# Attention nine pairs a group, and the eighth group's second product from seven products of quarters

## The chip, the cores and the metric

The kernel runs on one core of one Trainium2 chip. The metric is the device time of one execution in microseconds (us). Before the change it is 911.19 us, the median of three runs (911.01 to 911.4).

## The reference

Windowed attention (8 batches, 8 heads, 576 positions, head size 64), and then a SiLU MLP on its 4608 rows of 512 columns:

```python
scores = np.where((rel >= 0) & (rel < 128), q @ k.T / 8 + bias, -1e9)     # per batch and head
attn = exp(scores - max) / (sum + 1e-9)
x = (attn @ v).transpose(0, 2, 1, 3).reshape(4608, 512)
h = x @ w_in                      # 512 -> 2048
out = (h / (1 + exp(-h))) @ w_out # 2048 -> 512
```

## The kernel before

**Precision.** A float32 operand is carried as two fp16 parts (high and low), and a product is three matmuls: high by high, high by low, low by high. Such a matmul has a 128x128 block as its stationary operand and 512 columns as its moving operand.

**Groups and blocks.** The 4608 rows are nine groups of 512 (`g` from 0 to 8; "the eighth group" is `g` = 7). The 2048 hidden columns are 16 blocks of 128 (`f`); `n = 16 g + f` numbers all blocks. For each `n`, `gemm1` writes a PSUM tile `h` (12 matmuls), `act1` takes its tanh on ScalarE, `act2` forms the SiLU in the tile `gt` on VectorE, `act3` makes the high part `gh` on ScalarE, `act4` the low part `gl` on VectorE, and `gemm2` adds the block's share to four PSUM tiles `o` (12 matmuls). After the last block `store` sends the four tiles out.

**Steps.** `gemm1` and `gemm2` are cut into halves of six matmuls. Such a half is a step; a group has 64 steps. In this order the program issues for a block n: the two halves of `gemm1(n)`, then the two halves of `gemm2(n - 1)`. A table `plan`, filled by `put(step, function, ...)`, says what else is issued ahead of each step; `rank` sorts the work of one step. Each engine then runs its own queue strictly in the order in which the program issued it, and waits where a tile isn't ready.

**Attention.** A pair is half of the heads (four) for 128 rows; there are 72 pairs, p = 0 to 71, and a group needs eight of them before its MLP can begin. `at(p)` is the step at which pair p's `scores` are issued on TensorE. VectorE takes the row maxima (`row_max`, four instructions that also add the bias) in the next step, ScalarE the exponentials (`exps`) and their high part `hr` (`p_hi`), VectorE the low part (`p_lo`); two DMA transposes on SyncE's queue (`p_transpose`, tile `hl`) turn them, and `attend` is issued on TensorE 12 or 13 steps after the scores. `normalize` (three VectorE instructions), `x_hi` and `x_lo` follow, and `x_dma` transposes the finished rows `x`. From pair 36 on, q and k come as float32 (`load_qk16`, tile `r`, 512 KB) and are split by `hi16` on ScalarE and `lo16` on VectorE. Scores and attend share two PSUM buffers, called "a". In the pairs from 18 on `at(p)` is 8 steps a pair.

**Statistics.** The scale of each batch pair b = 2, 3 is taken from the data ahead of its first attention pair: nine blocks of v (`vscale_load`, `vscale_reduce` on VectorE) and nine of q and k (`qk_load`, `qk_sum`: two ScalarE sums each). Then `vscale_finish` runs in three stages.

**The last group.** The group in `FAST` takes its second product by seven products of quarters instead of eight (`gemm2_fast`): 512 rows by 128 hidden columns are seen as 2 x 2 quarters, which need sums and differences of activations (`act_sums`, three VectorE instructions per block) and of weights (`sum_float`, `sum_make`, `sum_hi`, `sum_lo`: eight blocks, mostly on GpSimd, in `SUMS_STEP` = 14 steps a block from step `SUMS` = 332). A block n is then 24 matmuls of 256 columns in `gemm1_fast` and 21 of 256 columns in `gemm2_fast`; `join_products` combines and `store_fast` sends out. Its `LAG` is two blocks: `gemm2(n - 2)` follows `gemm1(n)`. All other groups drain at their last block: `gemm2` of blocks 14 and 15 both run before the next group's first `gemm1`, with `turn_over` making `gh` and `gl` at once.

## Time and profile before

| | |
|---|---|
| median of three runs | 911.19 us |
| the profiled execution, its own time | 911.29 us |
| its span, first to last instruction | 909.5 us |
| TensorE (PE) busy | 900.5 us of the span |
| VectorE (DVE) busy | 718.6 us |
| ScalarE (ACT) busy | 582.9 us |
| GpSimd (POOL) busy | 180.8 us |

The 1.8 us between span and time lie around the program. Times in the rows are microseconds from the span's start, and nanoseconds where a mean of one instruction is given. PE's matmuls overlap their ends; the pace of a stream is read from one start to the next.

### The profile page before, as it was taken

The numbers are of one execution on the slowest core, as the hardware profiler recorded it, in microseconds if no ns is written. First come the engines' busy times: TensorE is split into PE (matmuls) and PEld (weight loads), VectorE is DVE, ScalarE is ACT, GpSimd is POOL, SyncE is SP. The second block draws the span as 40 slices with busy tenths as digits, with TensorE's granted clock in tenths as the row PEclk, the third lists the DMA queues.
The fourth block names the chain that finished last, engine by engine and source line by source line (L and its number), as shares of the span: only waits on it lengthen the run. The fifth ranks groups of instructions, "written<-read, shape, count | busy, mean of one in ns | idle before, by whom it ended". The sixth has DMA issues, their size and how long they took to land.

```text
span 909.5 us, 17946 instructions
## 1 busy us (share of the span) xinstructions
PE 900.5 (99%) x6761; PEld 570.0 (63%) x6761; DVE 718.6 (79%) x1734; ACT 582.9 (64%) x1184; POOL 180.8 (20%) x191
## 2 busy tenths in 40 slices
PE   9999999999999999999999999999999999999998
PEld 7877776888855555555555555555555555547887
DVE  6998998787988886767788888988988876655675
ACT  7789986675567755556577766666766666533342
POOL 2356662000000000000000004555654200000000
PEclk9999999999999999999999999999999999999999
DMA  8979824333386645434798736434655454311000
GB/s 324 395 178 258 242 55 132 71 93 71 82 234 162 184 117 125 112 90 116 171 248 204 197 93 155 105 93 105 163 116 117 116 154 107 78 35 59 1 25 24
DMA packets 198182, 122.94 MB, mean 135 GB/s; under 512 B 166480, under 2 KB 167632, under 8 KB 198096
## 3 DMA queue, kind: packets, MB, share of 16 engines
q1 hardware_dynamic: 197664, 121.41, 51.1%
q8 instruction: 53, 0.87, 0.4%
q10 hardware_dynamic: 432, 0.39, 0.1%
q14 instruction: 33, 0.27, 0.1%
HBM read 71.96 MB, written 9.44 MB: 89 GB/s over the span
## 4 chain that ended last, share of the span: by engine, by line
PE 81%; DVE 4%; ACT 2%; issue 1%; DVEq 0%; ACTq 0%
PE o L951 32%; PE h L754 30%; PE h L726 5%; PE av L584 4%; PE m L858 4%; PE sp L479 3%; PE sp L486 2%; PE h L759 1%; DVE hr L534 1%; DVE gt L787 1%; ACT gh L818 1%; DVE gl L832 1%; DVE t L510 1%; ACT t L520 0%; DVE x L155 0%
## 5 line engine op out<-in xcount | busy, mean ns | idle before, releaser
L754 PE MATMUL h<-xt,w 128*128 128x512 f16 (+1 forms) x1536 | 311.9, 353 | 0.0
L951 PE MATMUL o<-w,gh 128*128 128x512 f16 (+1 forms) x1024 | 311.1, 385 | 0.8 <-ACT gh L814 0.6
L783 ACT ACTIVATE gt<-h,tsc 128x512 f32<-128x512 f32 x128 | 87.7, 685 | 210.0 <-PE h L754 196.8
L754 PEld LDWEIGHTS <-w 128*128 128x128 f16 x1536 | 143.3, 98 | 123.1 <-issue 2.4
L951 PE MATMUL o<-w,gl 128*128 128x512 f16 (+1 forms) x512 | 196.3, 383 | 0.4 <-DVE gl L832 0.2
L787 DVE SCALAR_TENSOR_TENSOR gt<-gt,h 128x512 f32<-128x512 f32 x144 | 98.4, 684 | 79.1 <-ACT gt L783 78.5
L951 PEld LDWEIGHTS <-gh 128*128 128x128 f16 x768 | 74.6, 98 | 89.1 <-ACT gh L818 1.1
L520 ACT ACTIVATE t<-t,mx 128x256 f32<-128x256 f32 (+1 forms) x288 | 125.6, 485 | 7.4 <-DVE mx L510 7.2
L832 DVE SCALAR_TENSOR_TENSOR gl<-gt,wcut,gh 128x512 f16<-128x512 f32 x96 | 80.2, 835 | 52.4 <-ACT gh L818 51.6
L455 POOL TENSOR_SCALAR v<-rv,vsc 128x512 f16<-128x512 f32 x30 | 25.4, 848 | 471.1 <-DMA rv<-v 347.7
L534 DVE SCALAR_TENSOR_TENSOR hr<-t,hr 128x512 f16<-128x512 f32 (+1 forms) x128 | 97.0, 767 | 2.4 <-ACT hr L529 2.3
L818 ACT ACTIVATE gh<-gt,wcut 128x512 f16<-128x512 f32 x96 | 69.2, 721 | 39.0 <-DVE gt L787 36.1
L529 ACT ACTIVATE hr<-t 128x512 f16<-128x512 f32 (+1 forms) x128 | 71.3, 595 | 1.9 <-DMA hl<-hr 1.9
L951 PEld LDWEIGHTS <-gl 128*128 128x128 f16 x384 | 37.6, 98 | 46.7 <-DVE gl L832 1.8
L584 PEld LDWEIGHTS <-hl 128*128 128x128 f16 x1464 | 52.1, 98 | 15.9 <-issue 4.9
L510 DVE CUSTOM_DVE_ANT_0 t<-sp,tab,vsc 128x256 f32<-128x256 f32 (+1 forms) x144 | 58.5, 461 | 0.7
L584 PE MATMUL av<-v,hl 128*128 128x65 f16 (+1 forms) x1464 | 54.9, 193 | 1.7 <-DVE mx L510 1.0
L951 PEld LDWEIGHTS o<-w,gh 128*128 128x128 f32 x256 | 46.0, 188 | 10.3 <-issue 1.0
L510 DVE CUSTOM_DVE_ANT_0 t<-sp,tab 128x256 f32<-128x256 f32 (+1 forms) x144 | 50.1, 403 | 2.6 <-PE sp L486 2.3
L153 POOL TENSOR_TENSOR w<-wm,w 128x512 fp32r<-128x512 f32 x32 | 44.3, 1384 | 2.6
L759 PE MATMUL h<-xh,w 128*128 128x512 f32 x128 | 44.5, 404 | 0.0
L726 PE MATMUL h<-xt,w 128*128 128x256 f16 x384 | 44.2, 273 | 0.0
(193 smaller groups left out, 1232.3 us busy)
## 6 DMA issues: line engine op xcount, KB each, us to landing
r<-qk SPq DMA_DIRECT2D x36, 512.0 KB, 4.1
qs<-qk SPq DMA_DIRECT2D x18, 512.0 KB, 5.0
wr<-w_in SPq DMA_DIRECT2D x16, 512.0 KB, 6.8
wr<-w_out SPq DMA_DIRECT2D x16, 512.0 KB, 6.4
out<-ot SPq DMA_DIRECT2D x32, 256.0 KB, 2.6
rv<-v SPq DMA_DIRECT2D x30, 256.0 KB, 4.1
vm<-v SPq DMA_DIRECT2D x27, 256.0 KB, 4.7
q<-qk SPq DMA_DIRECT2D x18, 256.0 KB, 3.6
```

What stands on the lines that cost most here:

```text
L510: nc.vector.tensor_tensor_reduce(out=st[p]["t"][u][:, h, 2 * P - n :], in0=st[p]["sp"][h][:, u, o].rearrange("p o c -> p (o c)"), in1=tab[ ...
L520: nc.scalar.activation(x, x, AF.Exp, bias=st[p]["mx"][:, 2 * u + h : 2 * u + h + 1], scale=-1.0)
L529: nc.scalar.activation(split_of(p, u, hr)[:, 0], t[:, :, 2 * P - n :], AF.Copy, scale=PSCALE)
L534: nc.vector.scalar_tensor_tensor(out=hr[:, 1], in0=t[:, :, 2 * P - n :], scalar=PSCALE, in1=hr[:, 0], op0=ALU.mult, op1=ALU.subtract)
L584: nc.tensor.matmul(av[:, 2 * u + h, : rhs.shape[-1]], lhs, rhs, start=(n == 0), stop=(n == len(seq) - 1), skip_group_check=True,)
L726: nc.tensor.matmul(out, w[:, wp, cc], xt[g, "g"][:, 2 * t : 2 * t + 2, xp * NCC + cc], start=half == 0 and i == 0, stop=i == len(seq) - 1, ...
L754: nc.tensor.matmul(o, w[:, wp, cc], x, start=start and k == 0, stop=stop, skip_group_check=True)
L783: nc.scalar.activation(gt, hps[n], AF.Tanh, scale=scale)
L787: nc.vector.scalar_tensor_tensor(out=gt, in0=gt, scalar=1.0, in1=hps[n], op0=ALU.add, op1=ALU.mult)
L818: nc.scalar.activation(gh, gt, AF.Copy, scale=cut_of(n))
L832: nc.vector.scalar_tensor_tensor(out=gl, in0=gt, scalar=cut_of(n), in1=f32(gh) if n // NF < OUT16 else gh, op0=ALU.mult, op1=ALU.subtract)
L951: nc.tensor.matmul(ops[ti], a[:, t], w, start=(f == 0 and i == 0), stop=(f == NF - 1 and i == len(seq) - 1), skip_group_check=True,)
```

## The change

`FAST` gets the eighth group as well. Attention from pair 18 on runs nine pairs a group, at steps of seven (`PACE`, `EACH`); attend comes 10 steps after the scores (11 for a group's ninth pair). So attention ends in the seventh group. The weight sums start at step 240 instead of 332. The statistics of b = 2 and 3 stand at steps of four from 127 and 197 (`BOUNDS`, `FINISH`), and their nine reductions of v move from VectorE to ScalarE. Output tiles go to other buffers.

```diff
-FINISH1 = (37, 42, 45)
+FINISH = {1: (37, 42, 45), 2: (166, 168, 170), 3: (236, 239, 241)}
+BOUNDS = {2: 127, 3: 197}
-FAST = (NG - 1,)
+FAST = (NG - 2, NG - 1)
-SUMS, SUMS_STEP = 332, 14
+SUMS, SUMS_STEP = 240, 14
+OUT_TAGS = {3: ("w1_14", "w1_9"), 4: ("w1_13", "w1_14"), 6: ("w1_0", "w1_1")}
+PACE, EACH = 7, 9
...
-    return STEP * (p - 2 * GT) - LEAD
+    if p < 4 * GT + 2:
+        return STEP * (p - 2 * GT) - LEAD
+    g, k = divmod(p - 4 * GT - 2, EACH)
+    return (g + 1) * SLICE * NF + 2 + PACE * k
...
-        if b > 1 or b == 0 and i % 2:
+        if b == 0 and i % 2:
             nc.vector.tensor_reduce(m, t, axis=AX.XY, op=ALU.max, apply_absolute_value=True)
...
-            if n // NF == NG - 1:
-                act_sums(n)
+            act_sums(n)
...
-            a = n + (15 if p < 4 * GT else 13 if i < QK16 * NBLK else 12)
+            a = n + (15 if p < 4 * GT else 13 if p < 4 * GT + 2 else 11 if (p - 4 * GT - 2) % EACH == EACH - 1 else 10)
...
+        for b in range(QK16, NBB):
+            n = BOUNDS[b] + 4 * i
+            put(n, vscale_load, b, i)
+            put(n + 1, qk_load, b, i)
+            put(n + 4, vscale_reduce, b, i)
+            put(n + 6, qk_sum, b, i)
-            put(LOAD1[i // 2] if b == 1 else n - 53 + 5 * i, vscale_load, b, i)
-                put(n - 52 + 5 * i, qk_load, b, i)
-                put(n - 46 + 5 * i, qk_sum, b, i)
```

SyncE's queue around the transposes of pairs 48 and 49, before the change (`hl48_0` is the transposed probabilities of pair 48, `r16_51` the raw q and k of pair 51):

```order
L542 DMA_TRANSPOSE hl48_0_6913<-hr48_0_6887 128x8x128
L542 DMA_TRANSPOSE hl48_1_6953<-hr48_1_6910 128x8x128
L411 DMA r16_51_6966<-qk16 128x1024
L653 DMA_TRANSPOSE xt20_6029<-x23_6812 128x8x128
L542 DMA_TRANSPOSE hl49_0_7070<-hr49_0_7058 128x8x128
```

The same place after the change:

```order
L418 DMA r16_51_6763<-qk16 128x1024
L549 DMA_TRANSPOSE hl48_0_6782<-hr48_0_6736 128x8x128
L549 DMA_TRANSPOSE hl48_1_6797<-hr48_1_6779 128x8x128
L660 DMA_TRANSPOSE xt20_6205<-x23_6667 128x8x128
L418 DMA r16_52_6918<-qk16 128x1024
L549 DMA_TRANSPOSE hl49_0_6941<-hr49_0_6891 128x8x128
```

The raw load of a pair three later has moved from behind a pair's two transposes to ahead of them.

VectorE's queue in the stretch in which GpSimd makes the weight sums, before the change (`gt84` and `gl84` are `act2` and `act4` of block 84, `t52` the scores with bias of pair 52):

```order
L787 SCALAR_TENSOR_TENSOR gt84_7434<-gt84_7434,h84_7411 128x512
L832 SCALAR_TENSOR_TENSOR gl84_7452<-gt84_7434,wcut_3034,gh84_7451 128x512
L155 SCALAR_TENSOR_TENSOR x25_7455<-xs50_7421,x25_7455 128x256
L510 ISA t52_0_7495,mx52_7484<-sp52_0_7466,tab_65,vsc2_4578 128x256
L510 ISA mx52_7484 128x1
L510 ISA t52_1_7497,mx52_7484<-sp52_0_7466,tab_65,vsc2_4578 128x256
```

In that stretch after the change, at block 70 and pair 48:

```order
L794 SCALAR_TENSOR_TENSOR gt70_6703<-gt70_6703,h70_6671 128x512
L517 ISA t48_0_6706,mx48_6696<-sp48_0_6678,tab_65,vsc2_4448 128x256
L517 ISA mx48_6696 128x1
L517 ISA t48_1_6708,mx48_6696<-sp48_0_6678,tab_65,vsc2_4448 128x256
L517 ISA mx48_6696 128x1
L517 ISA t48_0_6706,mx48_6696<-sp48_1_6679,tab_65,vsc2_4448 128x256
L517 ISA mx48_6696 128x1
L517 ISA t48_1_6708,mx48_6696<-sp48_1_6679,tab_65,vsc2_4448 128x256
L517 ISA mx48_6696 128x1
L435 SCALAR_TENSOR_TENSOR q16_49_6645<-r16_49_6469,vsc2_4448,q16_49_6645 64x512
L838 SCALAR_TENSOR_TENSOR gl70_6722<-gt70_6703,wcut_3090,gh70_6721 128x512
```

Before, scores always fell on the same place within a block's four steps; with steps of seven they take all four places in turn. Here `act4` has moved away from `act2`, behind the four row maxima and a `lo16`.

## Rows read from the trace of the kernel before

**Rows 1.** The page: engines' busy time, and PE's granted clock in 40 slices.
```profile
PE 900.5 (99%) x6761; PEld 570.0 (63%) x6761; DVE 718.6 (79%) x1734; ACT 582.9 (64%) x1184; POOL 180.8 (20%) x191
...
PEclk9999999999999999999999999999999999999999
```

**Rows 2.** The page: the chain that ended last, by engine.
```profile
PE 81%; DVE 4%; ACT 2%; issue 1%; DVEq 0%; ACTq 0%
```

**Rows 3.** PE's own waits from the third to the eighth group, with their releasers.
```profile
PE o L951 <- ACT gh L818: 0.2, 1, 0.2
PE o L951 <- DVE gl L832: 0.2, 1, 0.2
```

**Rows 4.** Timeline of PE at the eighth group's end (start, us, what).
```profile
818.30 2.75 PE L754 MATMUL h<-xt,w 128*128 128x512 f16 x12
820.89 0.59 PE L951 MATMUL o<-w,gh 128*128 128x512 f16 x2
...
823.48 0.59 PE L951 MATMUL o<-w,gh 128*128 128x512 f16 x2
824.16 0.39 PE L951 MATMUL o<-w,gl 128*128 128x512 f16 x1
```

**Rows 5.** Timeline of the ninth group: the first product of two blocks in succession.
```profile
865.95 2.78 PE L726 MATMUL h<-xt,w 128*128 128x256 f16 x24
...
870.87 2.78 PE L726 MATMUL h<-xt,w 128*128 128x256 f16 x24
```

**Rows 6.** Busy time in windows: weight sums, fifth group, eighth group, twelve blocks of the ninth.
```profile
core 0: us, PE busy (x) PEld busy (x) DVE busy (x) ACT busy (x) POOL busy (x), PEclk, DMA share, GB/s
557.40:718.20 160.80, 160.38 (x1157) 83.44 (x1155) 141.01 (x294) 106.44 (x208) 84.92 (x84) 1.00 0.49 116
445.40:542.00 96.60, 96.60 (x711) 51.05 (x710) 79.14 (x204) 67.76 (x143) 2.93 (x4) 1.00 0.75 194
...
732.80:826.30 93.50, 93.42 (x649) 47.92 (x648) 59.95 (x145) 48.06 (x89) 2.80 (x3) 1.00 0.38 94
836.40:895.30 58.90, 58.90 (x542) 52.80 (x540) 41.20 (x83) 24.45 (x40) 0.00 (x0) 1.00 0.03 10
```

**Rows 7.** Timeline of SyncE's queue: the transposes of two pairs.
```profile
625.46 2.63 SPq L542 DMA_TRANSPOSE hl<-hr  x2
...
755.31 2.58 SPq L542 DMA_TRANSPOSE hl<-hr  x2
```

**Rows 8.** Timeline of PE: the attends that read them.
```profile
632.85 0.89 PE L584 MATMUL av<-v,hl 128*128 128x65 f16 x24
...
765.38 0.89 PE L584 MATMUL av<-v,hl 128*128 128x65 f16 x24
```

**Rows 9.** Tile hl in the stretch of the weight sums: its transposes, issue to landing.
```profile
DMA to landing us min/median/max: 2.3/2.7/4.4
```

**Rows 10.** VectorE's groups in that stretch (busy us, mean ns, idle before).
```profile
L832 DVE SCALAR_TENSOR_TENSOR gl<-gt,wcut,gh 128x512 f16<-128x512 f32 x27 | 27.3, 1011 | 13.6 <-ACT gh L818 13.3
...
L787 DVE SCALAR_TENSOR_TENSOR gt<-gt,h 128x512 f32<-128x512 f32 x27 | 18.4, 682 | 4.1 <-ACT gt L783 3.9
```

**Rows 11.** VectorE's groups in the eighth group, where GpSimd makes no sums.
```profile
L832 DVE SCALAR_TENSOR_TENSOR gl<-gt,wcut,gh 128x512 f16<-128x512 f32 x16 | 12.0, 751 | 8.2 <-ACT gh L818 8.0
L787 DVE SCALAR_TENSOR_TENSOR gt<-gt,h 128x512 f32<-128x512 f32 x16 | 11.0, 687 | 22.0 <-ACT gt L783 22.0
```

**Rows 12.** The statistics' instructions, whole run: q and k sums, v reductions.
```profile
L236 ACT ACTIVATE qs<-qs 128x512 f32<-128x512 f32 x36 | 22.1, 615 | 0.9 <-DMA qs<-qk 0.9
...
L217 DVE TENSOR_REDUCE vmx<-vm 128x1 f32<-128x512 f32 x18 | 12.2, 680 | 0.1
...
L236 ACT ACTIVATION_READ_ACCUMULATOR qs<-qs 128x1 f32 x36 | 6.7, 187 | 0.0
```

More of the change, by code (lines that the diff above doesn't have):

```diff
@@ L60 @@
 OWN = ("w1_12", "w1_13")
+OWN_FIRST = ("w0_15", "w0_14")
 FREE = ("w1_14", "w0_15", "w0_14", "w1_12", "w0_13")
-FINISH1 = (37, 42, 45)
+FINISH = {1: (37, 42, 45), 2: (166, 168, 170), 3: (236, 239, 241)}
+BOUNDS = {2: 127, 3: 197}
 LOAD1, REDUCE1 = (-9, -8, -6, -5, -4), (25, 21, 17, 13, 11)
@@ L203, in vscale_load @@
         else:
-            tag, bufs = ("rv", 2) if b == QK16 else (OWN[i % 2], 1)
+            tag, bufs = (OWN_FIRST if b == QK16 else OWN)[i % 2], 1
             t = pool.tile([P, DM], F32, tag=tag, bufs=bufs, name=f"vm{b}_{i}")
@@ L795, in act_sums @@
             return
-        engine, a = nc.vector if n // NF == NG - 1 else nc.gpsimd, gact[n]
+        engine, a = nc.vector, gact[n]
         pairs = a[:, 0:4].rearrange("p (a b) c -> p a b c", b=2)
@@ L838, in turn_over @@
         act2(n)
-        if n // NF in FAST and n // NF < NG - 1:
-            act_sums(n)
         act3(n)
@@ L855, in gemm2_fast @@
                 if j == 0 and side == 0 and a is gh:
-                    ops[b] = psum.tile([P, DM], F32, tag=("axaz" if n_last(g, t) else "wxyz")[b], bufs=2 if n_last(g, t) and b % 2 == 0 else 1, name=f"m{g}_{t}_{b}")
+                    ops[b] = psum.tile([P, DM], F32, tag=("axaz" if t else "wxyz")[b], bufs=2 if t and b % 2 == 0 else 1, name=f"m{g}_{t}_{b}")
                 for part in parts:
@@ L957, in store @@
         tag, bufs = ("x", 4) if ti > 1 else ("io", 2)
+        if ti > 1 and g > 2:
+            tag, bufs = (OUT_TAGS[g][ti % 2], 1) if g in OUT_TAGS else ("big", 2)
         ot = pool.tile([P, DM], F32, tag=tag, bufs=bufs, name=f"ot{g}_{ti}")
@@ L1159, in tile_window_attention_then_silu_mlp @@
             put(g * SLICE * NF - 12, mlp_scales, g)
-    for b in range(1, NBB):
-        n = at(2 * GT * (NBLK * b // GT)) + 2
-        for i in range(VCH):
-            put(LOAD1[i // 2] if b == 1 else n - 53 + 5 * i, vscale_load, b, i)
-            x = n - 49 + 5 * i
-            x += x % STEP == (7 if b == QK16 else 6)
-            put(REDUCE1[i // 2] + 2 * (i % 2) if b == 1 else x, vscale_reduce, b, i)
-            if b >= QK16:
-                put(n - 52 + 5 * i, qk_load, b, i)
-                put(n - 46 + 5 * i, qk_sum, b, i)
-        for x, wait in enumerate((0, 2, 5)):
-            put(FINISH1[x] if b == 1 else n + wait, vscale_finish, b, x)
+    for i in range(VCH):
+        put(LOAD1[i // 2], vscale_load, 1, i)
+        put(REDUCE1[i // 2] + 2 * (i % 2), vscale_reduce, 1, i)
+        for b in range(QK16, NBB):
[4 more added lines that the diff above has]
+            put(n + 6, qk_sum, b, i)
+    for b in range(1, NBB):
+        for x in range(3):
+            put(FINISH[b][x], vscale_finish, b, x)
     pos = [at(0)]
@@ L1198, in w_next @@
             later(1, w_next_load)
-    rank = {normalize: 0, in_scale: 2, out_scale: 2, vscale_finish: 2.5, act2: 1, act_sums: 1, act3: 1, act4: 1, other_batch: 2, row_max: 2, exps: 2, p_hi: 2, p_lo: 2, p_transpose: 2}
+    rank = {normalize: 0, in_scale: 2, out_scale: 2, vscale_finish: 2.5, act2: 1, act3: 1, act4: 1, other_batch: 2, row_max: 2, exps: 2, p_hi: 2, p_lo: 2, p_transpose: 2}
     FRONT = scores, other_batch, row_max
@@ L1279, in tile_window_attention_then_silu_mlp @@
                             turn_over(n)
-                        elif n // NF in FAST and n // NF < NG - 1:
-                            late = 4 if n % NF else 3
-                            ahead(late + 1, act4, n)
-                            ahead(late, act3, n)
-                            ahead(1, act_sums, n)
-                            ahead(1, act2, n)
                         else:
```

## The prediction

> **What bounds the kernel now.** I read the page first. TensorE is busy for 900.5 of 909.5 us, at a granted clock of full speed (2.4 GHz) in every slice [rows 1], and the chain that ended last is TensorE's for 81% [rows 2]. The waits say the same from the other side: from the third to the eighth group, 575 us, only two of PE's own waits are listed, 0.2 us each [rows 3]. So the time is the sum of what TensorE has to do. VectorE and ScalarE have slack, and cost nothing until a TensorE instruction comes to its turn before its operand is there. Two questions follow: how much shorter TensorE's stream becomes, and whether attention at nine pairs a group still arrives in time.
>
> The stream's price is read from its starts. At the end of the eighth group 12 matmuls of 512 columns go from 818.30 to 820.89, 2.59 us, 0.216 us each [rows 4]. These are two steps, so a step is 1.295 us, a block of four steps 5.18 us, and a group's 64 steps 82.9 us. In the ninth group one block (24 + 21 matmuls of 256 columns) goes from 865.95 to 870.87, 4.92 us, 0.109 us a matmul [rows 5].
>
> **What the change takes away.** The eighth group's 16 blocks go from 24 matmuls of 512 columns to 45 of 256: 16 x (5.18 - 4.92) = 4.2 us less. The eighth group also ends without draining into the ninth. There the starts at 823.48 and 824.16 lie 0.68 us apart where two matmuls take 0.43: a wait of 0.25 us for the last low part, which goes [rows 4]. What the seven products add on other engines is hidden: in twelve such blocks of the ninth group VectorE is busy for 41.2 and ScalarE for 24.5 of 58.9 us, and TensorE for all of it [rows 6]. The eighth group will look like that, since its attention is over; without that cover VectorE's 3.4 us a block would bound nothing either, being under 4.92. The two joins of the eighth group are of the same kind as the ninth group's first one, which lies inside the window without a gap in TensorE's time. Without any new wait the profiled time is 911.29 - 4.2 - 0.25 = 906.8 us.
>
> One rule of the Trainium skill speaks against the quarters. The page "TensorE: Matmul & The Clock Gate", section "Back-to-back issue gap", gives a stream of weight loads and matmuls 131 ns a matmul at 512 columns and 81 at 128; a line between them has 98 at 256. By it a block would go from 24 x 131 = 3.1 us to 45 x 98 = 4.4 us, as an estimate, and the change would add 20 us. This trace disagrees, with 216 and 109 ns [rows 4, 5], and decides.
>
> **What the change moves.** Attention's TensorE work is the same in sum: it only moves to earlier groups. What it can cost is waiting, at three places.
>
> *The stretch of the weight sums.* GpSimd's sums move from steps 332-438 to 240-346, and again run beside attention. In 27 blocks (108 steps) of that stretch now, 160.8 us, VectorE is busy for 141.0 us [rows 6]. An `act4` there takes 1011 ns, against 751 where GpSimd is idle, while `act2`, which reads one operand from PSUM, keeps 682 against 687 [rows 10, 11]: part of the load comes from GpSimd. TensorE's share: 108 x 1.295 = 139.9 us, which leaves 20.9 us for 13.5 pairs, 1.55 us a pair. With steps of seven there are 15.4 pairs, so 139.9 + 15.4 x 1.55 = 163.8 us. VectorE: `act2` and `act4` stay at 27.3 + 18.4 = 45.7 us [rows 10]; the other 95.3 us are 7.06 a pair, and 15.4 pairs are 108.7; together 154.4 us, 94% of 163.8. That leaves 9.4 us. Now VectorE idles there for 13.6 us ahead of `act4`, waiting for ScalarE's `gh`, and for 4.1 ahead of `act2` [rows 10]. If these waits stayed as they are, 154.4 + 13.6 + 4.1 = 172.1 us would be needed and TensorE would wait 8.3 us. I don't think they stay, because of the order: before, 14 of the 27 blocks have `act4` right behind `act2` on VectorE with nothing to fill the time, and after the change 6 of 27, the rest having row maxima, a `lo16`, a `p_lo` or a normalize between them. So 13.6 x 6/14 = 5.8, and 154.4 + 5.8 = 160.2 fits into 163.8 if the waits for the tanh give way, which they do where VectorE is late.
>
> *The attends.* Two transposes feed an attend. Without sums beside it, the pair at 755.31 issues its second one some 1.3 us later; at 2.7 us to landing it is there at 759.3, and the attend starts at 765.38: 6.1 us to spare [rows 7, 8, 9]. In the stretch of the sums the pair at 625.46 has its second one landed between 629.5 (2.7 us) and 631.2 (the stretch's longest, 4.4), and attends at 632.85: 3.4 to 1.7 us [rows 7 to 9]. The change takes two steps, 2.6 us, from each of these: 3.5 us stay without sums, 0.8 to -0.9 with them. The order on SyncE's queue worsens the second case, since the 512 KB load of raw q and k now goes ahead of the two transposes instead of behind. An attend that comes late holds TensorE, but the next pair's scores have then been issued, so that this pair gains the same time: at most every second pair pays, 15.4 / 2 x 0.9 = 6.9 us. These are not added to the 8.3 us, since a late VectorE is what makes transposes late. For the stretch the bounds are thus 0 and 8.3 us; I take 1.2, nearer to nothing, because the queue's order refills most of the idle time.
>
> *The two stretches of statistics.* Nine reductions of v (680 ns on VectorE) go to ScalarE, where I price them by the nearest row, the sums of q and k: 615 + 187 = 0.80 us [rows 12]. The fifth group shows ScalarE with one such stretch: 67.8 of 96.6 us, 18 x 0.80 = 14.4 of it the q and k sums [rows 6, 12]. The other 53.4 us in 64 steps become up to 60.0 with nine pairs. A stretch is now 36 steps instead of 45: 30.0 to 33.8 us of other work, 14.4 and 9 x 0.80 = 7.2, together 51.6 to 55.4 us, in 36 x 1.295 + 36/7 x 1.55 = 54.6 us of TensorE. So ScalarE is at 95 to 101%, against 52 of 67 us now. Queued behind a late sum are the next tanh and `gh`, and TensorE's `gemm2` waits for these. For both stretches the bounds are 0 and twice 0.8 + 4.6 (VectorE's idle time ahead of `act4`, 8.2 us in 16 blocks [rows 11], taken for nine blocks as ScalarE's own), 10.8 us. I take 0.8: the stretches are short, and a late tanh has some 2 us of TensorE's work ahead of it before anything waits: `gemm2(n)` comes two steps and 2.59 us of `gemm1` after the end of `h`, and the chain from tanh to `gl` is four instructions of 0.68 to 0.75 us.
>
> **The sum.** 911.29 - 4.2 - 0.25 + 1.2 + 0.8 = 908.8 us. The profiled run lies 0.1 us over the median of the three shown, so nothing is corrected for it.
>
> **The rivals.**
> - *Attention arrives in time everywhere*: 906.8 us. For it speaks that TensorE waits so little now, at 88% of VectorE in the stretch of the sums [rows 3, 6], and that the added load is refilled idle time. Against it, the two stretches of ScalarE at 95% and more.
> - *The waits eat the gain*: transposes behind the raw loads late in the stretch of the sums, at about half the upper bound (4.2 us), and the statistics at 1.0: 906.8 + 5.2 = 912.0. For it speak the 0.8 to -0.9 us above; against it, that most transposes there land in 2.7 us [rows 9].
> - *VectorE becomes the bound in the stretch of the sums*, which ends on the other side: if its waits for `gh` stay at 13.6 us, TensorE waits 8.3 us there, and with 0.8 for the statistics the time is 906.8 + 9.1 = 915.9. It decides from the point where VectorE's busy and waiting time pass 163.8 + 4.45 = 168.3 us, that is 13.9 us of waits where I count 5.8.
> - *The stream isn't shorter*, as the page's spacing has it (931 us): less than 1 in 100, since both forms of block are measured in this trace.
>
> **How the numbers follow.** What a measurement of this kernel can tell from no change is about 0.2%, 1.8 us: under 909.4 is faster, over 913.0 slower. The forecast, 907.6 to 909.4, has 0.33, and all in time 0.20; these two are the faster cases. The gain eaten, 909.4 to 913.0, has 0.27, and VectorE as the bound 0.20. So faster 0.53, same 0.27, slower 0.20. The range that leaves out no more than 2 in 10 is 906.4 to 913.0; its upper end leaves out the slower rival. The forecast's own range, with both signs so close, is 907.6 to 909.4.
>
> **What would show it.** In the changed kernel's trace the eighth group should be 16 blocks of 4.92 us, some 79 us, without attention, and with no gap of TensorE at its end. The seventh group and the ones before it should each be about 1.75 us longer than now. Waits of TensorE should stand in three places if anywhere: steps 240 to 346 (`attend` waiting for `hl` or for a row maximum, `gemm2` for `gl`), and the two stretches from 127 and 197 (`gemm2` for `gh` or `gl`, behind a late tanh). Transposes should land later than now. The prediction is wrong if these waits sum to more than 4.5 us, if the eighth group's blocks take longer than 4.92 us, or if TensorE waits elsewhere, as for an output tile's buffer or for the two stages of the scales that stand two steps apart now instead of three.

## The result, and the profile after

The changed kernel takes 924.5 us (median of four runs, 924.0 to 926.6) against 911.3 beside it: a ratio of 1.0149 (1.0132 to 1.0167), 1.5% slower. The forecast was 908.8, its own range 907.6 to 909.4, the wider one 906.4 to 913.0; the slowest rival was at 915.9. The profiled execution is the slowest of the four, 926.6 us with a span of 924.5. Its mean granted clock was 0.998 and that of the other three 1.000, so what its trace shows of a slower clock is not in the median.

The page of the changed kernel: busy times, and the chain that ended last by engine.

```profile
PE 902.6 (98%) x7097; PEld 603.3 (65%) x7097; DVE 736.8 (80%) x1791; ACT 605.7 (66%) x1236; POOL 183.4 (20%) x191
...
PE 65%; DVE 10%; DMA 6%; ACT 5%; issue 2%; SPq 1%; POOL 0%; DVEq 0%; POOLq 0%; ACTq 0%
```

PE's share of the chain fell from 81% [rows 2] to 65%; VectorE's rose from 4% to 10%, and the DMAs entered it with 6%. PE's own waits in the stretch 250 to 765 us (line, releaser, us in total, times, longest), where [rows 3] had two of 0.2 us:

```profile
PE av L591 <- DMA hl<-hr: 8.1, 9, 1.9
PE av L591 <- DVE mx L517: 3.5, 6, 0.9
PE vs L310 <- DVE r L609: 2.1, 1, 2.1
PE sp L486 <- DVE xs L618: 0.2, 1, 0.2
```

Attends (`av`) wait for transposed probabilities and for row maxima, and the matmul that spreads the scale (`vs`) for VectorE; together 13.9 us. The groups from the second to the ninth, from the first `gemm1` matmul of one to that of the next (windows of the changed kernel: us, then busy us and instructions of PE, PEld, DVE, ACT, POOL, PE's clock, DMA share, GB/s):

```profile
150.11:254.09 103.98, 103.93 (x901) 84.77 (x901) 87.53 (x226) 71.33 (x152) 4.04 (x5) 1.00 0.41 95
254.09:357.46 103.37, 101.58 (x750) 52.42 (x750) 79.58 (x214) 74.47 (x165) 2.90 (x4) 1.00 0.68 171
357.46:462.59 105.13, 99.04 (x710) 51.39 (x709) 81.66 (x202) 78.70 (x175) 19.49 (x20) 0.98 0.71 186
462.59:563.94 101.35, 98.72 (x745) 52.03 (x744) 89.33 (x196) 69.21 (x134) 54.50 (x51) 1.00 0.56 125
563.94:663.89 99.95, 96.79 (x706) 50.39 (x704) 82.55 (x190) 64.39 (x126) 25.04 (x25) 1.00 0.52 125
663.89:762.12 98.23, 97.73 (x746) 52.05 (x745) 76.69 (x194) 60.23 (x113) 2.95 (x4) 1.00 0.48 119
762.12:836.85 74.73, 74.73 (x703) 67.06 (x702) 52.18 (x110) 30.36 (x50) 0.00 (x0) 1.00 0.18 44
836.85:924.50 87.65, 83.68 (x767) 74.75 (x764) 57.98 (x116) 33.19 (x52) 0.00 (x0) 1.00 0.06 19
```

The same groups took 101.2, 99.6, 94.8, 96.6, 94.2, 96.6, 93.6 and 83.2 us before. A ninth pair is worth 1.55 us; what the second to seventh groups took beyond that is 1.2, 2.3, 8.8, 3.2, 4.2 and 0.1 us, 19.8 in sum. (The second group's 1.2 is not a wait: that group takes 104.0 us in run 13 too, which hardly waits.) The eighth and ninth groups together fell by 14.4: six pairs that left (9.3) and 5.1 for the products.

That gain came about as forecast, 4.2 + 0.25. The end of the eighth group on PE (start us, us, ...):

```profile
831.94 2.78 PE L733 MATMUL h<-xt,w 128*128 128x256 f16 x24
...
836.74 0.27 PE L862 MATMUL m<-wt,io 128*128 128x256 f16 x1
836.85 2.78 PE L733 MATMUL h<-xt,w 128*128 128x256 f16 x24
```

A block lasts 4.91 us, and the next group's first matmul follows its predecessor by 0.11 us: no drain. So the forecast was lost ahead of the eighth group, most of it in the attends. Two of them show how. The first is undisturbed, in the seventh group, with GpSimd nearly idle. PE and then VectorE around the scores of pair 66:

```profile
699.31 1.06 PE L486 MATMUL sp<-k,q 128*128 128x128 f16 x16
...
704.09 0.89 PE L591 MATMUL av<-v,hl 128*128 128x65 f16 x24
```

```profile
702.42 0.69 DVE L794 SCALAR_TENSOR_TENSOR gt<-gt,h 128x512 f32<-128x512 f32 x1 [2.64 <-ACT gt L790]
703.03 0.48 DVE L517 CUSTOM_DVE_ANT_0 t<-sp,tab,vsc 128x256 f32<-128x256 f32 x1
703.43 0.08 DVE L517 DVE_READ_ACCUMULATOR2_ANT mx<- 128x1 f32 x1
703.43 0.48 DVE L517 CUSTOM_DVE_ANT_0 t<-sp,tab,vsc 128x256 f32<-128x256 f32 x1
703.83 0.08 DVE L517 DVE_READ_ACCUMULATOR2_ANT mx<- 128x1 f32 x1
```

VectorE idles for 2.64 us in front of an `act2` that waits for its tanh, while the scores behind it in its queue have been there since 700.4. The row maxima (`t`, `mx`) begin 2.7 us after the scores' end, and the attend of pair 65, which takes the PSUM buffer of these scores, starts at 704.09, 0.18 us after the second maximum. Nothing waits, and hardly anything is to spare. What stands behind such maxima is late as well. ScalarE's waits for row maxima over the whole run, before and after:

```profile
ACT t L520 <- DVE mx L510: 7.2, 14, 3.1
...
ACT t L527 <- DVE mx L517: 36.3, 52, 3.1
```

The second is disturbed: pair 53, whose scores start at 554.29. SyncE's queue, and then PE:

```profile
564.87 1.23 SPq L549 DMA_TRANSPOSE hl<-hr  x1
566.15 0.58 SPq L418 DMA_DIRECT2D r<-qk  x1
566.77 0.90 SPq L977 DMA_DIRECT2D out<-ot  x2
567.78 1.75 SPq L549 DMA_TRANSPOSE hl<-hr  x1
```

```profile
570.99 0.52 PE L591 MATMUL av<-v,hl 128*128 128x65 f16 x12
573.25 0.54 PE L591 MATMUL av<-v,hl 128*128 128x65 f16 x12 [1.74 <-DMA hl<-hr]
```

The low parts were ready 10.5 and 12.1 us after the scores' start, the second transpose was issued behind a raw load and two output tiles and took 5.4 us to land, and the attend, eleven steps behind its scores (a group's ninth pair), waited 1.74 us for it.

### The profile page after: what moved, and what is told of

It reads as the page before. It is cut to its first block, busy times and chain, and to the rows that moved or that the text cites. A ratio compares the mean times of both kernels' runs of the same rounds, so it can differ in the third digit from the quotient of the medians.

```text
span 924.5 us, 18753 instructions
## 1 busy us (share of the span) xinstructions
PE 902.6 (98%) x7097; PEld 603.3 (65%) x7097; DVE 736.8 (80%) x1791; ACT 605.7 (66%) x1236; POOL 183.4 (20%) x191
## 4 chain that ended last, share of the span: by engine, by line
PE 65%; DVE 10%; DMA 6%; ACT 5%; issue 2%; SPq 1%; POOL 0%; DVEq 0%; POOLq 0%; ACTq 0%
PE o L955 20%; PE h L761 19%; PE h L733 9%; PE m L862 8%; DMA hl<-hr 4%; PE av L591 3%; PE sp L486 2%; DVE t L517 2%; PE sp L493 2%; PE h L766 1%; DVE gt L794 1%; DVE hr L541 1%; DVE gl L838 1%; ACT gh L824 1%; DVE k L435 1%
## 5 line engine op out<-in xcount | busy, mean ns | idle before, releaser
L955 PE MATMUL o<-w,gh 128*128 128x512 f16 (+1 forms) x896 | 273.6, 387 | 0.5 <-ACT gh L820 0.5
L761 PE MATMUL h<-xt,w 128*128 128x512 f16 (+1 forms) x1344 | 270.6, 350 | 0.0
L761 PEld LDWEIGHTS <-w 128*128 128x128 f16 x1344 | 127.4, 98 | 111.5 <-issue 4.9
L790 ACT ACTIVATE gt<-h,tsc 128x512 f32<-128x512 f32 x128 | 87.4, 683 | 133.3 <-PE h L761 105.1
L955 PE MATMUL o<-w,gl 128*128 128x512 f16 (+1 forms) x448 | 172.3, 385 | 0.1
L462 POOL TENSOR_SCALAR v<-rv,vsc 128x512 f16<-128x512 f32 x30 | 25.2, 838 | 463.0 <-DMA rv<-v 304.5
L955 PEld LDWEIGHTS <-gh 128*128 128x128 f16 x640 | 59.8, 98 | 65.1
L733 PE MATMUL h<-xt,w 128*128 128x256 f16 x768 | 88.9, 273 | 0.0
L838 DVE SCALAR_TENSOR_TENSOR gl<-gt,wcut,gh 128x512 f16<-128x512 f32 x80 | 63.4, 793 | 28.1 <-ACT gh L824 26.8
L824 ACT ACTIVATE gh<-gt,wcut 128x512 f16<-128x512 f32 x80 | 57.4, 718 | 43.3 <-DVE gt L794 42.7
L733 PEld LDWEIGHTS <-w 128*128 128x128 f16 x768 | 75.1, 98 | 8.9
L536 ACT ACTIVATE hr<-t 128x512 f16<-128x512 f32 (+1 forms) x128 | 73.8, 597 | 2.0 <-DMA hl<-hr 2.0
L955 PEld LDWEIGHTS <-gl 128*128 128x128 f16 x320 | 31.3, 98 | 38.1 <-DVE gl L838 0.4
L955 PEld LDWEIGHTS o<-w,gh 128*128 128x128 f32 x256 | 45.7, 188 | 10.5 <-issue 1.0
```

The source lines that it names most:

```text
L536: nc.scalar.activation(split_of(p, u, hr)[:, 0], t[:, :, 2 * P - n :], AF.Copy, scale=PSCALE)
L733: nc.tensor.matmul(out, w[:, wp, cc], xt[g, "g"][:, 2 * t : 2 * t + 2, xp * NCC + cc], start=half == 0 and i == 0, stop=i == len(seq) - 1, ...
L761: nc.tensor.matmul(o, w[:, wp, cc], x, start=start and k == 0, stop=stop, skip_group_check=True)
L790: nc.scalar.activation(gt, hps[n], AF.Tanh, scale=scale)
L838: nc.vector.scalar_tensor_tensor(out=gl, in0=gt, scalar=cut_of(n), in1=f32(gh) if n // NF < OUT16 else gh, op0=ALU.mult, op1=ALU.subtract)
L955: nc.tensor.matmul(ops[ti], a[:, t], w, start=(f == 0 and i == 0), stop=(f == NF - 1 and i == len(seq) - 1), skip_group_check=True,)
```

## The experiments

Each run is compared with runs of the kernel before on the same chip; ratios are to these.

**1 to 4.** My theory was the short lead: attends stand too early in TensorE's queue. The first two kernels move them, the third moves the raw loads, the fourth is the kernel before with the products alone.

```diff
-a = n + (15 if ... else 11 if (p - 4 * GT - 2) % EACH == EACH - 1 else 10)
+a = n + (15 if ... else 12 if (p - 4 * GT - 2) % EACH == EACH - 1 else 11)
```

> The changed kernel with every attend one step later: 11 steps after its scores (12 for a group's ninth pair). Theory 'short lead': the added time is TensorE waiting at attends that stand too early in its queue; each gains 1.3 us, so the nine waits for the transposes (8.1 us on the matmuls, 0.3 to 2.0 each) shrink to about 2 us and the nine for row maxima (4.4 us, at most 1.1 each) go; only the scale's 2.2 us and the slow matmuls behind it stay: 911 to 914 us. Rival 'load': at steps of seven VectorE and SyncE don't keep pace, and the waits move to the scores, which then wait for the normalize behind the later attend: 920 us or more. Rival 'raw loads' (transposes late because the 512 KB loads stand ahead of them on SyncE's queue): the same as 'short lead' here for waits under 1.3 us; told apart by the run that moves the loads.

Measured: 928.7 us, 1.0195 (1.018 to 1.021), slower still, the number of the rival "load". PE's longest waits between 250 and 765 us:

```profile
PE sp L486 <- DVE xs L618: 10.9, 9, 2.2
PE o L955 <- DVE gl L838: 2.0, 3, 1.5
PE vs L310 <- DVE row L307: 2.0, 1, 2.0
PE sp L493 <- DVE xs L618: 1.4, 1, 1.4
```

No attend waits there. Scores do, for the normalize (`xs`) of the pair two earlier. The longest of these on VectorE, and then on PE:

```profile
590.25 1.28 DVE L838 SCALAR_TENSOR_TENSOR gl<-gt,wcut,gh 128x512 f16<-128x512 f32 x1 [0.79 <-ACT gh L824]
591.46 0.94 DVE L541 SCALAR_TENSOR_TENSOR hr<-t,hr 128x256 f16<-128x256 f32 x1
592.33 0.21 DVE L607 TENSOR_SCALAR r<-av,unit 128x4 f32<-128x4 f32 x1
592.57 0.18 DVE L610 RECIPROCAL r<-r 128x4 f32<-128x4 f32 x1
592.78 0.42 DVE L618 TENSOR_TENSOR xs<-av,r 128x256 f32<-128x256 f32 x1
```

```profile
590.81 0.28 PE L486 MATMUL sp<-k,q 128*128 128x128 f16 x2
593.27 0.95 PE L486 MATMUL sp<-k,q 128*128 128x128 f16 x14 [2.18 <-DVE xs L618]
```

The normalize stands behind an `act4` that waits for `gh` and a low part of the probabilities, and the scores' second half waits for the buffer of the attend.

```diff
-a = n + (15 if ... else 11 if (p - 4 * GT - 2) % EACH == EACH - 1 else 10)
+a = n + (15 if ... else 13 if (p - 4 * GT - 2) % EACH == EACH - 1 else 12)
```

> The changed kernel with every attend two steps later, 12 after its scores (13 for a ninth pair), the lead of before, at the pace of seven. Theory 'short lead': no wait for transposes or row maxima stays, but the scores two pairs later stand only two steps behind the attend whose buffer they take: about 0.4 us stays of the 3.0 us that lie between a normalize and those scores, so scores begin to wait in about a third of the pairs, 0.3 us each: 910 to 915 us, near the run with 11. Rival 'load': scores wait in nearly all pairs, 920 us and more.

Measured: 957.4 us, 1.0506 (1.048 to 1.0532); scores waited for `xs` for 25.3 us in 20 places of the same stretch. The theory fell in this form: a later attend only hands the wait on.

```diff
-put(n - 18, load_qk16, p)
+put(n - 16, load_qk16, p)
```

> The changed kernel with only the raw loads of q and k two steps later (16 instead of 18 ahead of the scores), so that they stand behind a pair's two transposes on SyncE's queue, as before the change. Rival 'raw loads': the hl waits from the fourth group on (some 8 us) go, 915 to 917 us. Theory 'short lead': transposes land late for other reasons as well (late row maxima, late low parts), the attends of the third group had the same waits with no raw load in sight; the time falls by 3 us at most: 921 to 924.5 us.

Measured: 927.8 us, 1.0184 (1.0167 to 1.0201). The waits for `hl` fell to 1.6 us, those for row maxima rose to 7.5, and the time, above both numbers, is no shorter. With the old order on SyncE's queue others wait.

```diff
-FAST = (NG - 1,)
+FAST = (NG - 2, NG - 1)
```

> The kernel before with only the eighth group added to FAST: attention stays at eight pairs a group and eight steps, and still runs beside the eighth group's blocks; the sums stay at step 332, those of its activations go to GpSimd there. If the seven products bring 4.2 us a group and the drain 0.25, and nothing else is touched: 906.8 us (ratio 0.995). Rival: with attention beside them the faster blocks make VectorE the bound in the eighth group (two blocks and a pair last 2 x 4.92 + 1.55 = 11.4 us on TensorE; VectorE's two blocks without the sums 2 x 1.5 and a pair 5 to 7 us fit, with GpSimd sharing its port not surely), and 1 to 4 us of waits eat the gain: 908 to 911.

Measured: 925.4 us, 1.0155 (1.0138 to 1.0172). The groups up to the seventh were as before, the eighth and ninth took 14.2 us more: waits for `xs` (8.0 us), for a low part at the start of the ninth group (3.3), for row maxima (1.8). That is over both numbers. So in this form the products can't be had beside attention at steps of eight; the kernel before makes their activation sums on GpSimd there, and no other form was tried.

**5 to 8.** The second theory was the place in the block. The first two issue the row maxima, and then the low parts, earlier; the other two put the lead of ten steps, and then the bad place, into the kernel before.

```diff
-put(n + 1, row_max, p, 0)
-put(n + 1, row_max, p, 1)
+put(n + (p < 4 * GT + 2), row_max, p, 0)
+put(n + (p < 4 * GT + 2), row_max, p, 1)
...
+if w[0] in FRONT:
+    return 3 + 0.1 * FRONT.index(w[0])
```

The last two lines keep scores ahead of their maxima, both last in their step; runs 6, 9, 10, 17 and 18 have them too.

> The changed kernel with the row maxima issued in the step of their scores instead of the next one (pairs from 18 on), leads as changed. Theory 'place in the block': with steps of seven the scores fall on all four places of a block; on two of them the row maxima stand on VectorE behind act2 or act4, which wait there for a tanh or a gh (2.66 and 2.0 us after the scores even where nothing else disturbs, against 0.4 on the place that all pairs had before). Issued a step earlier they stand ahead of these: the waits for row maxima (4.4 us) go, and low parts and transposes come 1 to 2 us earlier, so that most of the 10 us of waits for hl go; the scale's 2.2 us and the 1.5 us of slow matmuls behind it stay: 911 to 917 us. Rival 'load' (VectorE at 78 to 88% of the longer groups can't keep the pace, wherever its work stands): 921 us or more.

Measured: 922.4 us, 1.0124 (1.0109 to 1.014), the rival's number. The waits for row maxima went, those for `hl` stayed at 6.0 us, and 3.2 us for `gl` came, since at a group's start `act4` now stood behind the maxima.

```diff
-put(n + 4 + late + u * (1 + more), p_lo, p, u)
-put(n + 4 + late + u * (1 + more), p_transpose, p, u)
+put(n + 4 + late + u * (1 + more) * (p < 4 * GT + 2), p_lo, p, u)
+put(n + 4 + late + u * (1 + more) * (p < 4 * GT + 2), p_transpose, p, u)
...
-FINISH = {..., 3: (236, 239, 241)}
+FINISH = {..., 3: (236, 242, 248)}
```

> The kernel of the run before (row maxima in the scores' step) with both low parts and transposes of a pair in one step (4 behind the scores; the second was at 5) and the last two stages of the scales of b = 3 at 242 and 248 instead of 239 and 241. Theory 'place in the block': the second low part no longer stands behind an act2 or act4 that waits, its transposes land up to 1.3 us earlier, and the wait of the scale's matmul with the slow matmuls behind it (3.7 us) goes: 3 to 6 us less than the run before, 907 to 912. Rival 'load': only the scale's 3.7 us.

Measured: 921.1 us (919.1 to 925.1), 1.0116 (1.0089 to 1.0142). In the profiled execution, at 925.1, the waits for `hl` are down to 0.2 us; `gl` took 4.7, and scores waited 2.8 us for a scale stage that holds their buffer. Neither theory's number came.

```diff
-a = n + (15 if p < 4 * GT else 13 if i < QK16 * NBLK else 12)
+a = n + (15 if p < 4 * GT else 13 if p < 4 * GT + 2 else 10)
```

> The kernel before with its attends 10 steps after the scores from pair 18 on (12 or 13 before), at steps of eight, where all pairs keep their one place in the block. Theory 'place in the block': 2.6 us less of a spare that was 3 to 6 us outside the stretch of the sums; waits only where less was left (some eight pairs in the two stretches with statistics or sums, 1 us each at most): 912 to 916 us. Rival 'short lead alone': the waits of the changed kernel, some 15 us: 920 us and more.

Measured: 921.9 us, 1.0113 (1.0097 to 1.013), the rival's number, but not by its mechanism: transposes made 0.4 us of waits and row maxima 7.2. At steps of eight an attend ten steps behind its scores is only two behind the next pair's.

```diff
-LEAD = 14
+LEAD = 13
```

> As the run before, with every pair's scores one step later (LEAD = 13), so that all row maxima stand behind an act2 that waits for its tanh. Theory 'place in the block': the row maxima begin 2.7 us after the scores instead of 0 to 0.4, the spare falls by another 2 us, and waits appear in most pairs from 18 on: 5 to 15 us more than the run before. Rival 'load' or 'short lead alone': the same as the run before within 2 us.

Measured: 1000.2 us, 1.0982 (1.0965 to 1.0998). PE's waits between 250 and 765 us, and VectorE at one of them:

```profile
PE av L584 <- DVE mx L510: 50.5, 37, 2.6
```

```profile
400.85 0.69 DVE L787 SCALAR_TENSOR_TENSOR gt<-gt,h 128x512 f32<-128x512 f32 x1 [3.43 <-ACT gt L783]
401.46 0.42 DVE L510 CUSTOM_DVE_ANT_0 t<-sp,tab 128x256 f32<-128x256 f32 x1
```

With the lead held, standing one step later is worth 78 us, five times my upper figure. Over the whole run the maxima make 71.9 us of waits instead of 8.3, and the mean granted clock is 0.987 instead of 1.000. All of attention's work moves with its scores, so it is the place of the whole chain in the block that this shows, with two steps between the next pair's scores and an attend; the changed kernel has three.

**9 to 12.** Repairs by place, one at a time, and the sums elsewhere.

```diff
+soon = p >= 4 * GT + 2 and n % 4 in (0, 3)
-put(n + 1, row_max, p, 0)
+put(n + 1 - soon, row_max, p, 0)
...
-put(n + 4 + late + u * (1 + more), p_lo, p, u)
+put(n + 4 + late + u * (1 + more) * (not soon), p_lo, p, u)
...
-FINISH = {..., 3: (236, 239, 241)}
+FINISH = {..., 3: (237, 240, 247)}
```

> The changed kernel; only where scores fall on the two bad places of a block (their row maxima would stand behind an act2 or act4 that waits), the row maxima are issued in the scores' step and both low parts 4 steps behind the scores; and the scale stages of b = 3 stand at 237, 240 and 247. Against the run with all pairs moved it leaves the low parts of a group's first block ahead of the row maxima. If the waits come from the place in the block and the two crowded stages: no hl waits over 0.5 us, no wait at the scale's matmul, none for gl at a group's second block: 911 to 915 us. If VectorE's load is what remains: 918 us and more, with the waits at other instructions.

Measured: 920.8 us, 1.0104 (1.0087 to 1.0121), the second number; with run 6, from which it can't be told apart, the fastest at steps of seven that computes everything. 6.2 us of waits for row maxima and 2.4 for `hl` stayed, mostly in the first four blocks of a group.

> The run before with the raw loads 16 instead of 18 steps ahead of the scores, behind a pair's two transposes on SyncE's queue. If the order of that queue matters once low parts come in time: transposes issued next to a raw load land in 2.7 us instead of 4 to 5, 1 to 3 us less than the run before; if the landing time comes from the load's traffic itself: the same within 1 us.

Its edit is that of run 3. Measured: 925.4 us, 1.0154 (1.0139 to 1.0169); waits for row maxima 10.9 us, for `hl` 0.5. That is 4.6 us more than run 9, which neither sentence had; why the maxima then wait longer was not followed up.

```diff
-FAST = (NG - 2, NG - 1)
-SUMS, SUMS_STEP = 240, 14
+FAST = (NG - 1,)
+SUMS, SUMS_STEP = 332, 14
```

> The changed kernel with only the ninth group in FAST and the weight sums back at step 332: attention alone at nine pairs a group, GpSimd quiet from step 240 to 331. If the sums beside attention cost what the changed kernel loses in the fifth and sixth groups (101.4 and 100.0 us against 96.6 and 94.2 with 8 pairs), the fifth falls to 98.1 (96.6 and 1.55 for the ninth pair) and the waits move to the sixth and seventh; if the pace of seven steps is what costs, the fifth stays at 100 us or more. As a whole 4.4 us more than the changed kernel for the products that it gives up: 926 to 930 us.

Measured: 928.2 us, 1.019 (1.0175 to 1.0205), as a whole as expected, with the fifth group between its two numbers. The fourth and fifth groups took 100.6 and 99.4 us instead of 105.1 and 101.4, 6.4 us less, with the scale's wait of 2.1 us and the slow matmuls behind it among what went; the seventh, now beside the sums, 104.3 instead of 98.2. The last two groups took 167.2 us against 162.4.

> The changed kernel with only the scale stages of b = 3 at 237, 240 and 247 instead of 236, 239 and 241. The 2.2 us wait of the scale's matmul for the row that VectorE makes, and 1.5 us of matmuls at half the clock behind it, go: 924.5 - 3.7 = 920.8 us. If the pairs behind it wait for the same VectorE work instead: 923 to 925 us.

Measured: 926.4 us, 1.0168 (1.0153 to 1.0183), above both numbers. The scale's wait went, and an attend behind it waited 3.1 us for `hl`.

**13 to 15.** These ask what the waits come from, by taking one thing out.

```diff
-st[p]["hl"][u] = hl = pool.tile([P, 8, P], F16, tag="hl", bufs=4, name=f"hl{p}_{u}")
-nc.sync.dma_start_transpose(hl[:, : 4 * n], hr[:, : 4 * n * P])
+st[p]["hl"][u] = hr.rearrange("p (a r) -> p a r", r=P)
```

The tile `hr` then takes the four buffers of `hl` instead of its own two.

> The changed kernel with the DMA transposes of the probabilities left out from pair 18 on: an attend reads the untransposed tile, with the same matmuls, and waits for the low part instead of a landed transpose (the output then lacks the transposition). If the landing time (2.7 to 5.5 us a transpose) is what makes attends late: the waits for hl, about 10 us, go; those for row maxima and the scale (8 us) stay: 913 to 916 us. If the loop of scores, row maxima, attend and normalize through the two PSUM buffers is as tight by itself, waits for row maxima take their place: 918 us and more.

Measured: 908.1 us, 0.9963 (0.9951 to 0.9976), under both numbers. PE's waits between 250 and 765 us:

```profile
PE o L954 <- DVE gl L837: 0.6, 1, 0.6
PE vt L293 <- DVE mx L517: 0.6, 1, 0.6
PE av L590 <- DVE mx L517: 0.2, 1, 0.2
PE av L590 <- ACT t L527: 0.2, 1, 0.2
```

Nearly all of it goes, 16.4 us, the waits for row maxima with it. These came, then, in a stream that late transposes had already pushed out of step, or from the two buffers of `hr`, which a late transpose keeps. The run doesn't part the two, but the changed kernel's trace speaks against the buffers: between 250 and 765 us it lists no wait of ScalarE for one. Late maxima alone don't make TensorE wait either: ScalarE waits for them as long here (26.6 us in that stretch, 25.2 in the changed kernel). A third possibility stays: the run also takes the transposes' traffic away (the DMA engines' share in the fifth group is 0.29 instead of 0.56) and empties SyncE's queue for the other loads.

```diff
+if n // NF > OUT16:
+    return
 nc.vector.scalar_tensor_tensor(
...
-seq = [(gh, hi), (gh, lo), (gl, hi)]
+seq = [(gh, hi), (gh, lo), (gh if g > OUT16 else gl, hi)]
```

> The changed kernel without act4 in the fourth to seventh group: gemm2's third matmul reads the high part again instead of a low part (the output then lacks the activations' low part there). It takes 0.75 us and one wait for gh off VectorE in each of 64 blocks. If VectorE's load and order make row maxima and low parts late: the waits of these four groups, 17 us, fall below 6, and the time to 911 to 914 us. If latencies of the chain that VectorE's load doesn't set (transposes, tanh, PSUM buffers) are the cause: 919 us and more.

Measured: 914.9 us, 1.0044 (1.0027 to 1.0061). PE's waits in the same stretch:

```profile
PE av L591 <- DMA hl<-hr: 3.9, 7, 1.1
PE av L591 <- DVE mx L517: 1.4, 2, 1.1
PE vs L310 <- DVE r L609: 1.0, 1, 1.0
```

Both time and waits (6.3 us) lie just over the first sentence's. A lighter VectorE shortens the same chain, by 9.6 us of time. Both of its shares, the 0.75 us and the wait for `gh`, went together.

```diff
-PACE, EACH = 7, 9
+PACE, EACH = 8, 8
-FAST = (NG - 2, NG - 1)
+FAST = (NG - 1,)
...
-a = n + (15 if ... else 11 if (p - 4 * GT - 2) % EACH == EACH - 1 else 10)
+a = n + (15 if ... else 12)
```

> The changed kernel with PACE and EACH at 8, attends 12 steps behind the scores, and only the ninth group in FAST (a raw-load buffer kept from the output tiles): what stays of the change are the statistics at steps of four on ScalarE, the crowded scale stages, the sums from step 240 and the moved output tiles. If the pace of seven, with its short lead, is the cause: 911 to 912.5 us, as the kernel before. If the other edits cost by themselves, as my terms for the sums and the statistics had it: 913 us and more, with the waits in steps 127 to 346.

Measured: 920.8 us, 1.0106 (1.0091 to 1.0121), the second number, and most of it in its place. From 250 us on no attend waited for transposes or maxima. The third group lost 6.3 us at scale stages (2.4, 1.3 and 1.0 us of waits, and matmuls at half the clock), since moved pairs met fixed stages.

**16 to 18.** The stages put right, and two last attempts at steps of seven.

```diff
-FINISH = {1: (37, 42, 45), 2: (166, 168, 170), 3: (236, 239, 241)}
+FINISH = {1: (37, 42, 45), 2: (172, 174, 177), 3: (244, 246, 249)}
```

> The run at steps of eight with all other edits, its scale stages moved to stand to the pairs as they do in the kernel before (172, 174, 177 and 244, 246, 249). In that run the third group had 6 us of waits at the stages. If the pace of seven and its lead are the cause, and the other edits cost little: 912 to 915 us (4 us were left in the fourth and sixth groups). If the statistics on ScalarE cost by themselves: 917 us and more.

Measured: 917.4 us, 1.0068 (1.0053 to 1.0083), the second number, but not by its mechanism. The third group is at 99.2 us, 0.4 under that of before, statistics on ScalarE included; the fifth and seventh, 95.8 each, are 0.8 under. The fourth now loses 7.1 us at its stages (101.9 against 94.8), 2.3 and 1.2 us of waits and matmuls at half the clock behind them; scores waited 1.3 us at the start of the sixth, which is 1.9 longer. So the other edits cost nothing that the trace shows, but for the scale stages and one wait of scores; these made 6.3 us here without steps of seven.

```diff
-SUMS, SUMS_STEP = 240, 14
+SUMS, SUMS_STEP = 250, 23
...
-a = n + (15 if ... else 11 if (p - 4 * GT - 2) % EACH == EACH - 1 else 10)
+a = n + (15 if ... else 12 if (p - 4 * GT - 2) % EACH == EACH - 1 else 10)
```

> The run that moved row maxima and low parts on the two bad places (920.8 us), with the attend of a group's ninth pair 12 instead of 11 steps behind its scores and the weight sums thinned: a block every 23 steps from 250 instead of every 14 from 240. Its waits of 2.6, 1.8, 1.1 us at the first pairs of the groups and 2.4 us at the start of the sums should shrink: 914 to 918 us. If the waits only move, as in the runs before: 919 us and more.

Measured: 921.8 us, 1.0121 (1.0104 to 1.0138), the second number: 6.4 us of waits for row maxima, one of them 3.0 us in the seventh group, where the sums now reach.

```diff
-put(2 if p == 2 * GT else n + 2, exps, p, 0)
-put(2 if p == 2 * GT else n + 3, exps, p, 1)
+put(2 if p == 2 * GT else n + 2 - soon, exps, p, 0)
+put(2 if p == 2 * GT else n + 3 - soon, exps, p, 1)
-late = 2 * (p == 2 * GT + 2)
+late = 2 * (p == 2 * GT + 2) - soon
```

> The run beside it with exponentials, high and low parts and transposes also one step earlier for the pairs on the two bad places. If the engines' order is what sets the chain's length, its transposes land up to 1.3 us earlier and another 2 to 4 us go: 911 to 915 us. If ScalarE then waits for row maxima and holds up the tanh behind it: no gain, or a loss.

Measured: 925.4 us, 1.0153 (1.0138 to 1.0168), a loss, as the second sentence had it. Row maxima made 8.4 us of waits, `xs` 3.5, `gh` 1.5. No version that computes everything beat the kernel before.

## Why the prediction was wrong

**What the change takes away: right.** A block is 4.91 us, the drain is gone, and the last two groups are 4.9 us shorter than those of run 11, which has the same attention and only one group of products. The page "TensorE: Matmul & The Clock Gate" of the Trainium skill, section "Back-to-back issue gap", by whose spacing the new block would have been the longer one, stays contradicted: 4.91 us for 45 matmuls are 0.109 us each.

**Without waits: right.** The term sum without waits was 906.8; run 13, whose attends hardly wait, is at 908.1. So of the 17.7 us between 906.8 and 924.5 all but 1.3 go with the transposes: the miss is waiting.

**The attends: here it failed.** The step was "The change takes two steps, 2.6 us, from each of these: 3.5 us stay without sums", with "at most every second pair pays" behind it, and so only 1.2 us for the stretch of the sums and none for attends elsewhere. All but 0.5 us of the listed waits stand in the stretch of the sums and the two of statistics, where I had looked for them; but they are 13.9 us instead of 2.0, and in the stretches of statistics attends waited (2.0 us for `hl`, 1.6 for row maxima), not `gemm2`. Two things were wrong in the step. I took the spare of pairs that all stood on one place of the block, and kept the rest of the chain as it was. At steps of seven six of a group's nine pairs stand elsewhere, four of them on the two places where the row maxima stand behind an `act2` or `act4` that waits: undisturbed, the pair at 699.31 had maxima that began at 703.03, and its second transpose, issued at 709.76, took 3.4 us to land, 1.6 us ahead of its attend at 714.77 where I had 3.5. How much the place can matter is shown by run 8. And I looked at one side of the attend only. An attend takes the PSUM buffer of the next pair's scores once their row maxima are read, and the scores after those take the attend's once it is normalized. Attend and normalize lie between two pairs' scores, and of the distance, now seven steps instead of eight, a share goes to each side. At eight steps it was four and four (five and three up to pair 35). Now it is three and four; four and three (run 1) and five and two (run 2) gave 4 and 33 us more, and two and six at the old pace (run 7) 10.9 more than before. None of the three leads at steps of seven was without waits, so the short lead can't be mended by moving the attend alone. Run 13 keeps these places and distances and hardly waits, so what is too tight is the two together with the transposes. How tight the chain is shows in what relieves it: 16.4 us without the transposes, 9.6 without `act4`, 2 to 4 for moving work earlier (runs 5, 6, 9; the last two moved scale stages too).

**The stretch of the weight sums: the size was off.** I took 1.2 from bounds of 0 and 8.3. The 27 blocks from step 240 on (a window as above, and VectorE's `act2` in it: busy us, mean ns, idle before):

```profile
428.19:606.00 177.81, 167.99 (x1238) 87.32 (x1237) 156.03 (x346) 117.09 (x228) 92.48 (x87) 0.99 0.53 121
...
L794 DVE SCALAR_TENSOR_TENSOR gt<-gt,h 128x512 f32<-128x512 f32 x27 | 18.4, 681 | 11.9 <-ACT gt L790 11.8
```

They took 177.8 us where I had 163.8. VectorE's load was as forecast, 156.0 us against 154.4, and its wait ahead of `act4` fell to 7.4 us (I had 5.8). But the wait for the tanh ahead of `act2`, which I let give way, rose from 4.1 [rows 10] to 11.9, and on one place of the block row maxima stand behind it. So VectorE was not full; it stood idle ahead of work that others waited for. (Part of this idling can be TensorE's waits coming back, since a late `h` makes a late tanh; the rows don't part that.) The sums' share is smaller than these 14 us: run 11 freed the fourth and fifth groups of them, and they fell by 6.4, the scale's wait included.

**The statistics: the place was wrong.** I took 0.8 us for late tanhs behind ScalarE's sums, with ScalarE at 95 to 101%. It was busy for 50.5 of 59.0 us in the second stretch (364 to 423), 86%, and no late tanh shows: between 250 and 765 us the changed kernel lists no wait of `gemm2` for `gh` or `gl`, and in run 16 the third group, with them, is 0.4 us faster than before. What cost is what I had only named as a possible error, the scale stages two steps apart: one wait of 2.1 us and, in the profiled execution, the matmuls behind it at half the clock. The runs that moved the stages, or the pairs against them (6, 12, 15, 16), each found another wait of 2 us or more near them; run 9, with the stages of run 12 and earlier maxima, none over 0.7.

**What would show it: half right.** In the stretch of the sums the waits did stand as `attend` waiting for `hl` or a row maximum. As a whole transposes did not land slower (median from issue to landing 2.8 us between 250 and 765, 2.7 before): they were issued later against their attend. Single ones were slow on top of that, as pair 53's second with 5.4 us.

What stays open: how the 16.4 us divide between the landing itself, the late state that it leaves on the queues behind it, and the traffic and queue that run 13 empties; and whether a differently ordered VectorE queue could hold seven steps. That the slack is gone in the orders tried is shown; that no order has it is not.

## What to carry to other kernels

Before a software pipeline is tightened, price its loop through each shared buffer on both sides of the instruction that is moved, and on every place that the new period visits; a spare read from one phase of the old period says little. An in-order engine that idles in front of a wait isn't slack for what stands behind that wait. When a repair of one wait makes another of like size, take a whole latency out, as an experiment, before trying a third order.

## What the runs showed of the hardware

A wait of TensorE can cost more than itself. After the scale's wait of 2.1 us in the profiled execution of the changed kernel the granted clock fell to half, 1.2 GHz, for a while; after two attends' waits of 1.9 and 1.7 us it didn't. The stretches behind these three waits (windows, columns as above):

```profile
437.83:440.30 2.47, 2.47 (x7) 0.91 (x6) 2.44 (x5) 0.93 (x3) 0.00 (x0) 0.50 0.47 106
458.50:461.50 3.00, 3.00 (x25) 1.48 (x23) 2.87 (x7) 2.65 (x7) 2.29 (x3) 1.00 0.00 1
573.70:577.00 3.30, 3.30 (x19) 1.48 (x16) 1.89 (x6) 1.51 (x4) 0.00 (x0) 1.00 1.24 141
```

In the first the matmuls of 512 columns are 0.43 us apart instead of 0.216, and by that some 1.5 us are lost, an estimate. VectorE's instructions with two operands in SBUF were much longer beside GpSimd's sums: a low part of the probabilities took 0.68 us at 696.95 and 1.15 at 553.23, and one of v 1.64 us at 555.77:

```profile
553.23 1.15 DVE L541 SCALAR_TENSOR_TENSOR hr<-t,hr 128x512 f16<-128x512 f32 x1
...
555.77 1.64 DVE L468 SCALAR_TENSOR_TENSOR v<-rv,vsc,v 128x512 f16<-128x512 f32 x1
```

This agrees with the Trainium skill, page "SBUF — State Buffer", section "SBUF: two separate sides": VectorE and GpSimd share a pair of ports as an exclusive lock, for VectorE among others when it reads two operands from SBUF against a GpSimd instruction that reads SBUF too. The trace shows the longer times, not the lock itself.
